# Weight loads moved into the middle of pair 14, and a second expert's turn inside the first up product, in a fused attention and expert kernel

## The chip, the cores and the metric

The kernel runs on one core of one Trainium2 chip. The metric is the device time of a whole execution in microseconds (us), the median of several runs. The profile is of one execution; its span, from the first to the last instruction, is a little shorter than the device time.

Names used below: TensorE (PE in the profile; PEld are its weight loads), VectorE (DVE), ScalarE (ACT), GpSimd (POOL), SyncE (SP). SBUF is the on-chip memory, PSUM holds the results of TensorE, DRAM is the memory outside.

## The reference

Two stages, cut to what matters here. First, attention with chunks selected per query, over 4 batches, 8 heads, 768 positions and a head size of 64; then a layer of 8 experts, each of which serves at most 80 tokens.

```python
# attention: q, k, v are (4, 8, 768, 64)
ub = upper bound of q.k over each chunk of 32 keys      # from k_min, k_max
sel = the 6 chunks with the largest ub, causal
attn = softmax(where(sel & causal, q @ k.T / 8, -1e9))
x = (attn @ v) as rows of 512, one for each of 3072 tokens

# experts: w_gate (512, 8), w1 (8, 512, 1024), w2 (8, 1024, 512)
expert_idx = argmax(x @ w_gate); gate_w = its softmax probability
out = zeros(3072, 512)
for e in range(8):
    tok_idx = tokens with expert_idx == e
    if more than 80: keep the 80 with the largest gate_w
    h = maximum(x[tok_idx] @ w1[e], 0)                  # "up"
    out[tok_idx] = gate_w[tok_idx] * (h @ w2[e])        # "down"
```

## The kernel before

Attention is worked off in 16 pairs of heads (`NP = 16`), numbered 0 to 15; four pairs make a batch. Beside the attention of one batch the kernel ranks the tokens of the batch before by their gate weight, so that after pair 15 only the last batch's ranking is left. Then come the experts. A helper `op(engine, instruction, r=..., w=...)` records what each instruction reads and writes and places the semaphore waits. Every engine works off its own instructions in program order; `"gpd"` is a DMA issued by GpSimd, `"sp"` one issued by SyncE.

The loop over pairs, cut to the order of the parts:

```python
for i in range(NP):
    kk, bb = i % NPB, i // NPB - 1      # NPB = 4; pair 14: kk = 2
    live = bb >= 0
    scores(i, 0, 2)                     # score products, exp
    ...
    folds(i, 0, 1)                      # GpSimd: causal select, adds into ES
    ...
    scores(i, 2, 4)                     # calls folds for steps 2 and 3
    if live and kk == 2:
        rank_count(bb)                  # TensorE; reads flags kept in w1s[7], w2s[6]
        rank_slot(bb)
    ...
    rows(i - 1); scale_rows(i - 1)      # token rows of pair i-1 to DRAM (x_rows)
    ...
    scores(i, 4, 6)                     # calls folds for steps 4 and 5
    ...
    values(i)                           # values product; reads steps 0,1,2,4 then 3,1,4,2,5
    if i == NP - 2:
        table(bb); merge(bb); vw_turn()
    ...
    if i == NP - 2:                     # pair 14
        wload(E - 2, 0); wload(E - 2, 1); wload(E - 1, 0)
    elif i > 1:
        wload((i - 2) // 2, i % 2)
    if i in (0, 1, 12, 13):             # zeros for a quarter of out
        ...                             # i == 0: clear the start of w1s[6]
        op("sp", lambda: sp.dma_start(zd, zs), r=[zk], w=[f"outz{g}"], ...)
```

`wload(e, 0)` loads w1 of expert e (f32 in DRAM, bf16 in SBUF, 1 MB written), `wload(e, 1)` its w2. The output's zeros are read out of a cleared part of `w1s[6]`, so w1 of expert 6 may be loaded only when the four zero writes are done. The ranking of a batch keeps flags in the buffers of w1 of expert 7 and w2 of expert 6 (`Cs`), so those may be loaded only when `rank_count` of pair 14 is done. w2 of expert 7 (`last_w2`) goes in eight pieces into buffers of q and k, and is issued near the end of pair 15.

The values product, and the selects that it waits for:

```python
# values: (key tile, first and last query, step, column)
AVS = [
  [(0, 0, 128, None, 0), (0, 128, 512, 0, 128), (1, 128, 512, 1, 0),
   (2, 256, 512, 2, 0), (3, 384, 512, 4, 0)],
  [(0, 512, 768, 3, 0), (1, 512, 640, 1, 384), (1, 640, 768, 4, 384), (2, 512, 768, 2, 256),
   (4, 512, 768, 3, 256), (3, 512, 768, 4, 128), (5, 640, 768, 5, 0)],
]
# folds: GpSimd clears the part of the diagonal above the causal line, then adds
op("gp", lambda: gp.affine_select(ad, a, ...), r=[f"E{st}"], w=[ak])          # line 544
op("gp", lambda: gp.tensor_tensor(o, in0, in1, ALU.add), ...)                 # line 553
```

After pair 15, the end of the last ranking and the experts:

```python
rows(NP - 1)
keep_warm(4)                      # four products of no use, 128 x 512 bf16
...
scale_rows(NP - 1)                # VectorE, then SyncE: last write to x_rows
gate_gcols(b)
last_count((0, 5, 1, 4, 2, 3), (0, 0, 0, 0, 0, 4))    # 2nd list: warming products after each
rank_slot(b); rank_hot(b); ...
table(b); merge(b)                # gives idx, the token indices of each expert
for e in range(3):
    gather(e)                     # GpSimd: 80 rows of x_rows by idx; waits for all writes
spread()
...
keep_warm(13)
turn(0)                           # TensorE transposes the 80 rows, ScalarE copies
gather(3)
up(0)
turn(1)
gather(4)
for e in range(1, E):
    if 1 < e + 1 < E:
        turn(e + 1)
        if e + 4 < E: gather(e + 4)
    up(e)                         # two halves of 16 products each
    if e % 4 > 0 and e != 3: down(e // 4 * 3 + e % 4 - 1)
    elif e == 4: down(2)
```

Of the kernel before, what the change touches and what calls it, by code (L numbers as in the profile page):

```python
# [5 lines left out]
ACTF = mybir.ActivationFunctionType  # L6
# [141 lines left out]
def bass_quest_chunk_select__then__topk_capacity_drop_kernel(  # L148
# [11 lines left out]
    E = moe_w_gate.shape[1]  # L160
    Fd = moe_w1.shape[2]
    Dm = moe_w_gate.shape[0]
    CAP = int(moe_capacity)
# [3 lines left out]
    DB = Dm // 128  # L167
    FB = Fd // 128
    NPB = H // 2
    NP = B * NPB  # L170
# [35 lines left out]
    with ExitStack() as pers:  # L206
# [15 lines left out]
        op = sy.op  # L222

        with nc.Block() as blk:

            @blk.sync
            def _body(_unused):
                sp = nc.sync
                gp = nc.gpsimd
                ve = nc.vector  # L230
                ac = nc.scalar
# [102 lines left out]
                def xTv(e):  # L334
                    return bass.AP(rq, (e % 2) * 160, [[S, 128], [1, 160]]).bitcast(BF16)
# [587 lines left out]
                for i in range(NP):  # L923
                    kk, bb = i % NPB, i // NPB - 1
                    live = bb >= 0
                    scores(i, 0, 2)
                    if i == NP - 1:
                        sort_rows(True)
                        vw_mm()
                        clear_xg("k", 0)  # L930
                    if i:
                        sums(i - 1)
                        scale_lg(i - 1)
                    folds(i, 0, 1)
                    if live and kk == 0:
                        gate_in(bb)
                    if live and kk == 1:
                        rank_pred()
                        rank_cmp(bb, 5)
                    scores(i, 2, 4)  # L940
                    if i == 0:
                        take_r(1)
                    if live and kk == 2:
                        rank_count(bb)
                        rank_slot(bb)
                    if live and kk == 3 and i < NP - 1:
                        table(bb)
                        merge(bb)
                    if i == 12:
                        sort_apply()  # L950
                        sort_take()
                    if i:
                        if i == NP - 1:
                            sort_rank(0)
                        rows(i - 1)
                        scale_rows(i - 1)
                    if i == NP - 2:
                        rank_late(bb)
                    if live and kk == 0:
                        gate_exp()  # L960
                        gate(bb)
                    scores(i, 4, 6)
                    if i + 1 < NP:
                        bounds(i + 1)
                    if i + 2 < NP:
                        take_q(i + 2)
                        take_r(i + 2)
                    if i + 1 < NP:
                        bounds_out(i + 1)
                    if i + 2 < NP:  # L970
                        take_k(i + 2)
                    if i + 4 < NP:
                        load(i + 4, "qk")
                    if i == NP - 4:
                        load_vk(NP - 1, 0)
                    if live and kk == 0:
                        rank_own(bb)
                    if live and kk == 1:
                        rank_diag(bb)
                        rank_cmp(bb, 4, 3, 2, 1, 0)  # L980
                    if live and kk == 2 and i < NP - 2:
                        rank_late(bb)
                    if i == NP - 1:
                        sort_rank(1)
                        last_w2()
                        break
                    if i == NP - 2:
                        op("dve", lambda: ve.tensor_scalar(triM[:], triQ[:], 1.0, 3e38, ALU.is_ge, ALU.mult), r=["triQ"], w=["triM"])
                        op("dve", lambda: ve.scalar_tensor_tensor(triM[:], ident_f[:], 3e38, triM[:], ALU.mult, ALU.max),
                           r=["triM", "ident_f"], w=["triM"])  # L990
                        for n, s in (("q", 0), ("q", 1), ("k", 1)):
                            clear_xg(n, s)
                    values(i)
                    if i == NP - 2:
                        table(bb)
                        merge(bb)
                        vw_turn()
                    if i + 2 < NP:
                        load(i + 2, "v")
                    if i + 1 < NP:  # L1000
                        unselT(i + 1)
                    if live and kk == 0:
                        rank_row(bb)
                    if i == 11:
                        sort_rows(False)
                        sort_rank()
                    if i == NP - 2:
                        wload(E - 2, 0)
                        wload(E - 2, 1)
                        wload(E - 1, 0)  # L1010
                    elif i > 1:
                        wload((i - 2) // 2, i % 2)
                    if i in (0, 1, 12, 13):
                        zk = f"w1_{E - 2}"
                        if i == 0:
                            op("dve", lambda: ve.memset(bass.AP(w1s[E - 2], 0, [[DB * Fd, 128], [1, 2 * Dm]]), 0.0), w=[zk])
                        g = (0, 1, 12, 13).index(i)
                        zs = bass.AP(w1s[E - 2], 0, [[DB * Fd, 128], [0, NT], [1, 2 * Dm]]).bitcast(F32)
                        zd = bass.AP(out.tensor, out.offset + g * NT * 128 * Dm, [[Dm, 128], [128 * Dm, NT], [1, Dm]])
                        op("sp", lambda: sp.dma_start(zd, zs), r=[zk], w=[f"outz{g}"], dsem=f"d_zero{g}")  # L1020
# [29 lines left out]
                last_high(2)  # L1050
                scale_rows(NP - 1)
                gate_gcols(b)
                last_count((0, 5, 1, 4, 2, 3), (0, 0, 0, 0, 0, 4))
                rank_slot(b)
                rank_hot(b)
                op("dve", lambda: ve.tensor_copy(dT[:, 2, :], gT[:]), r=["gT", "dT"], w=["dT"])
# [25 lines left out]
                        bounds_check=NTOK - 1, oob_is_err=False),  # L1082
                        r=XD + ["idx"] + ([f"xS{e - 3}"] if e > 2 else []), w=[xgk(e)], dsem=f"d_g{e}")

                def turn(e):
                    tp = MB if e % 2 == 0 else M0b
                    tk = "MB" if e % 2 == 0 else "M0"
                    for d in range(DB):
                        op("pe", lambda: pe.transpose(tp[:, d * CAP:(d + 1) * CAP], xgv(e)[:, ts(d)], ident_bf[0:CAP, 0:CAP]),
                           r=[xgk(e), "ident_bf"], w=[tk], inc=(d == DB - 1))  # L1090
                    k0 = ["rq"] if e < 2 else []
                    op("act", lambda: ac.activation(xTv(e), tp[:, 0:DB * CAP], ACTF.Copy), r=[tk], w=[f"xT{e % 2}", f"xS{e}"] + k0)

                def up(e):
                    s = e % 2
                    for hf in range(2):
                        for fb in range(hf * 4, hf * 4 + 4):
                            for d in range(DB):
                                o = SC[s][:, hf * 512 + (fb % 4) * CAP:hf * 512 + (fb % 4 + 1) * CAP]
                                op("pe", lambda: pe.matmul(o, w1s[e][:, d, ts(fb)], xTv(e)[:, d * CAP:(d + 1) * CAP],  # L1100
                                                           start=(d == 0), stop=(d == DB - 1)),
                                   r=[f"w1_{e}", f"xT{s}"], w=[f"H{s}{hf}", f"SC{s}"], inc=(fb % 4 == 3 and d == DB - 1))
                        src = SC[s][:, hf * 512:hf * 512 + 4 * CAP].rearrange('p (f c) -> p f c', f=4)
                        dst = hTv(e)[:, hf * 4 * HW:(hf + 1) * 4 * HW].rearrange('p (f c) -> p f c', f=4)[:, :, 0:CAP]
                        k0 = [("qT", "kT")[e // 2] + str(s)] if e < 4 and hf == 0 else []
                        if hf == 0:
                            op("act", lambda: ac.activation(dst, src, ACTF.Relu), r=[f"H{s}{hf}"], w=[f"hT{e % 4}{hf}"] + k0)
                        else:
                            op("dve", lambda: ve.tensor_scalar(dst, src, 0.0, None, ALU.max), r=[f"H{s}{hf}"], w=[f"hT{e % 4}{hf}"])
# [21 lines left out]

                for e in range(3):
                    gather(e)
                spread()
                for e in range(4):
                    t = (qT, kT)[e // 2 % 2][e % 2]
                    op("dve", lambda: ve.memset(bass.AP(t, CAP // 2, [[S, 128], [HW // 2, FB], [1, (HW - CAP) // 2]]), 0.0), w=[("qT", "kT")[e // 2] + str(e % 2)])
                keep_warm(13)
                turn(0)
                gather(3)  # L1140
                up(0)
                turn(1)
                gather(4)
                for e in range(1, E):
                    if 1 < e + 1 < E:
# [44 lines left out]
```

## Time and profile before

| | |
|---|---|
| device time, median of 3 runs | 297.52 us (297.23 to 298.48) |
| span of the profiled execution | 296.4 us |
| TensorE busy | 276.3 us (93%) |
| GpSimd busy | 227.3 us (77%) |
| VectorE busy | 210.4 us (71%) |
| ScalarE busy | 146.7 us (49%) |
| chain that ended last | TensorE 65%, GpSimd 15%, VectorE 10%, DMA 5% |
| bytes moved by DMA | 47.95 MB, 162 GB/s on average |

How to read it: the busy shares are averages over a long attention stage and a tail of experts, which have different limits. A second part of the profile page cuts the span into 40 equal slices, 7.41 us each, and gives each engine's busy share in tenths; a line PEclk gives the clock granted to TensorE in tenths of full speed, and a line DMA the busy share of the 16 DMA engines. The chain of waits follows the execution back from its last instruction to what released each step. L553 is line 553 of the kernel before; where one name stands for numbered buffers, the number is left out (`ES`, `EXB`, `w1s`). A DMA's "us to landing" is from its issue to the arrival of its last byte.

### The profile page before, as it was taken

The page shows a single profiled execution, that of the slowest core. Times are in us where ns is not written, and L with a number is a line of the kernel's source. Part 1 is how long each engine was busy: PE and PEld are TensorE (multiplying, and loading weights), DVE is VectorE, ACT ScalarE, POOL GpSimd, SP SyncE. Part 2 cuts the span into 40 slices and gives each one's busy share as a digit, 9 for nine tenths or more (in the row PEclk, how much of TensorE's full clock was granted, in tenths as well). Part 3 has the DMA queues.
Part 4 walks back from the last instruction along what each step waited for, and adds up shares of the span by engine and source line. Part 5 has one row for each costly group of instructions (what it writes and reads, how often), then busy time and mean ns, then how long its engine had stood idle before and what let it go on. Part 6 is the DMA issues. An engine that isn't in the chain of part 4 may idle for free.

```text
span 296.4 us, 8664 instructions
## 1 busy us (share of the span) xinstructions
PE 276.3 (93%) x3593; PEld 170.5 (58%) x3593; DVE 210.4 (71%) x573; ACT 146.7 (49%) x202; POOL 227.3 (77%) x297
## 2 busy tenths in 40 slices
PE   7579999999999999999999999999999999749992
PEld 7235565655656565656565656565656575327761
DVE  3767282737797989659889898898899989602431
ACT  2155646565657555545754546566656545103320
POOL 5039897989998999989899999899999924043522
PEclk9779999999999999999999999999999999877998
DMA  9997959699999899979899999997999699911211
GB/s 150 173 163 123 300 101 303 117 173 170 158 169 191 146 170 155 192 133 167 156 192 168 163 166 205 152 171 131 215 317 211 92 192 203 201 41 38 80 62 58
DMA packets 158359, 47.95 MB, mean 162 GB/s; under 512 B 142405, under 2 KB 150721, under 8 KB 158320
## 3 DMA queue, kind: packets, MB, share of 16 engines
q1 hardware_dynamic: 141664, 28.34, 48.3%
q0 software_dynamic: 13520, 18.67, 37.9%
q10 hardware_dynamic: 3136, 0.39, 0.9%
q8 instruction: 28, 0.46, 0.6%
q14 instruction: 11, 0.09, 0.1%
HBM read 53.49 MB, written 11.01 MB: 218 GB/s over the span
## 4 chain that ended last, share of the span: by engine, by line
PE 65%; POOL 15%; DVE 10%; DMA 5%; issue 2%; ACTq 1%; POOLq 0%; ACT 0%; DVEq 0%
PE SC L510 20%; PE OB L567 17%; POOL ES L553 12%; PE SC L525 4%; PE SC L1100 4%; PE M L594 4%; PE OB L1122 4%; PE OB L640 3%; DMA x_rows<-xp 3%; POOL EXB L544 3%; PE M L473 2%; PE M L580 2%; DMA kn<-in_k_dram 1%; PE MB L498 1%; DMA qn<-x_rows,idx 1%
## 5 line engine op out<-in xcount | busy, mean ns | idle before, releaser
L530 ACT ACTIVATE EXB<-SC 128x1024 f32<-128x1024 f32 x96 | 86.2, 916 | 49.4 <-PE SC L525 48.2
L553 POOL TENSOR_TENSOR ES<-ES,EXB 128x256 f32<-128x256 f32 (+1 forms) x105 | 101.6, 980 | 4.8
L510 PE MATMUL SC<-qT,kT 64*128 64x512 f32 (+3 forms) x512 | 99.2, 478 | 1.0 <-ACT EXB L530 1.0
L567 PE MATMUL OB<-EXB,vn 128*64 128x256 f32 (+3 forms) x704 | 72.8, 361 | 0.5 <-POOL EXB L544 0.5
L567 PEld LDWEIGHTS OB<-EXB,vn 128*64 128x64 f32 x704 | 46.6, 137 | 23.9 <-issue 9.5
L510 PEld LDWEIGHTS SC<-qT,kT 64*128 64x128 f32 x512 | 42.5, 191 | 25.2 <-issue 15.7
L553 POOL TENSOR_TENSOR ES<-EXB 128x768 f32<-128x768 f32 (+1 forms) x30 | 46.7, 1558 | 2.5
L525 PE MATMUL SC<-unsT,ind 64*128 64x128 bf16 (+5 forms) x256 | 38.2, 293 | 0.8 <-ACT unsT L500 0.8
L544 POOL TENSOR_SCALAR_AFFINE_SELECT EXB<-EXB 128x256 f32<-128x256 f32 x79 | 33.9, 439 | 2.5 <-ACT EXB L530 2.5
L575 ACT ACTIVATE oT<-OB 128x512 f32<-128x512 f32 (+1 forms) x32 | 15.6, 488 | 39.6 <-PE OB L567 39.6
L525 PEld LDWEIGHTS SC<-unsT,ind 64*128 64x128 bf16 x256 | 13.0, 96 | 18.5 <-issue 8.3
L441 DVE STREAM_TRANSPOSE qT<-qn 128x768 f32<-128x768 f32 x16 | 15.6, 972 | 9.2 <-PE SC L525 9.2
L585 DVE STREAM_TRANSPOSE M<-M 128x192 f32<-128x192 f32 x16 | 6.3, 394 | 21.8 <-PE M L594 21.5
L660 DVE TENSOR_TENSOR xp<-OB,rden 128x768 bf16<-128x768 f32 x16 | 15.3, 955 | 6.6 <-PE OB L640 6.3
L445 ACT ACTIVATE rq<-qT 128x768 f32<-128x768 f32 x16 | 13.5, 843 | 9.7 <-DVE qT L441 9.1
L451 DVE STREAM_TRANSPOSE kT<-kn 128x768 f32<-128x768 f32 x16 | 15.5, 967 | 3.6 <-DMA kn<-in_k_dram 3.6
L1080 POOL DMA_INDIRECT qn<-x_rows,idx x4 | 3.9, 980 | 17.4 <-DMA x_rows<-xp 14.6
L455 DVE TENSOR_REDUCE kmm<-kT 128x24 f32<-128x768 f32 x16 | 15.2, 950 | 0.5
L1128 POOL DMA_INDIRECT out_dram<-EXB,idR x6 | 6.0, 992 | 12.4 <-DVE EXB L1126 8.9
L457 POOL TENSOR_TENSOR kmm<-kmx,kmm 128x24 f32<-128x24 f32 x16 | 7.3, 454 | 10.7 <-DVE wg L904 7.0
L456 DVE TENSOR_REDUCE kmx<-kT 128x24 f32<-128x768 f32 x16 | 15.1, 942 | 0.0
L487 DVE MAX8 top<-M 128x8 f32<-128x8 f32 (+4 forms) x160 | 14.6, 166 | 0.6
(218 smaller groups left out, 417.6 us busy)
## 6 DMA issues: line engine op xcount, KB each, us to landing
w1s<-in_moe_w_dram POOLq DMA_DIRECT2D x8, 1024.0 KB, 10.1
w2s<-in_moe_w_dram POOLq DMA_DIRECT2D x7, 1024.0 KB, 11.2
qn<-in_q_dram SPq DMA_DIRECT2D x64, 96.0 KB, 3.0
vn<-in_v_dram SPq DMA_DIRECT2D x32, 192.0 KB, 3.9
out_dram<-w1s SPq DMA_DIRECT2D x4, 1536.0 KB, 7.8
kn<-in_k_dram SPq DMA_DIRECT2D x60, 96.0 KB, 2.6
x_rows<-xp SPq DMA_DIRECT2D x16, 192.0 KB, 6.4
kn<-in_k_dram ACTq DMA_DIRECT2D x4, 96.0 KB, 4.0
```

The costliest lines, as they stand in the source:

```text
L441: op("dve", lambda: ve.transpose(qT[j][:], qn[s][:].rearrange("p a b c -> p (a b c)")), r=[f"qn{s}{g}" for g in range(4)], w=[f"qT{j}"])
L451: op("dve", lambda: ve.transpose(kT[j][:], kn[s][:].rearrange("p a b c -> p (a b c)")), r=[f"kn{s}{g}" for g in range(4)], w=[f"kT{j}"])
L455: op("dve", lambda: ve.tensor_reduce(kmm[j][:, 0, 0:NCH], kv, AX, ALU.min), r=[f"kT{j}"], w=[f"kmm{j}"])
L456: op("dve", lambda: ve.tensor_reduce(kmx[:], kv, AX, ALU.max), r=[f"kT{j}"], w=["kmx"])
L510: op("pe", lambda: pe.matmul(o, kT[j][pr, ts(kt)], qT[j][pr, q0:q1], start=True, stop=False), r=[f"kT{j}", f"qT{j}"], w=[f"SC{s}"], inc=False)
L525: op("pe", lambda: pe.matmul(o, ind[pr, ts(kt)], unsT[j][pr, b0 - 128:q1 - 128], start=False, stop=True), r=[f"ind{h}", f"unsT{j}"], w=[f" ...
L530: op("act", lambda: ac.activation(Ex(st, None, 0, W), src, ACTF.Exp, scale=SCALE), r=[f"SC{s}"], w=[f"E{st}"])
L544: op("gp", lambda: gp.affine_select(ad, a, pattern=[[0, 2], [1, 128]], compare_op=ALU.is_ge, fill=0.0, base=0, channel_multiplier=-1), r=[ ...
L553: op("gp", lambda: gp.tensor_tensor(o, in0, in1, ALU.add), r=[f"E{s2}", f"E{first[0]}"] if first else [f"E{s2}"] + kt, w=kt)
L567: op("pe", lambda: pe.matmul(OB[pr, q0:q1], vn[s][:, kt, h, :], ex, start=(n == 0), stop=last), r=[f"vn{s}{h}", "ES0" if st is None else f ...
L575: op("act", lambda: ac.activation(oT[:, q0:q1], OB[:, q0:q1], ACTF.Copy), r=[f"O{bk}"], w=[f"oT{bk}"])
L660: op("dve", lambda: ve.tensor_tensor(xo, xi, rx, ALU.mult), r=["O0", "O1", "rden"], w=[f"xp{i % 2}"])
```

## The change

Four things are changed.

- The three weight loads of pair 14 (w1 and w2 of expert 6, w1 of expert 7) are issued right behind `rank_count`, in the middle of the pair, instead of at its end. They are meant to be out of the way of the last write of token rows. On GpSimd they now stand ahead of the selects of steps 4 and 5 and the six last adds of pair 14, instead of behind them.
- So that w1 of expert 6 finds its buffer free then, the zero writes go out in pairs 0, 1, 11 and 12 instead of 0, 1, 12 and 13. The part of the buffer that holds the zeros is untouched until then.
- The warming products are set anew: six instead of four after the last count, four new ones between table and spread, twelve instead of thirteen behind the spread, two new ones behind the first turn. They keep TensorE busy while it waits.
- The second expert's turn goes into the middle of the first up product, and VectorE instead of ScalarE copies its result to SBUF, so that TensorE doesn't wait for that copy.

The diff, with the parts cut that only carry these through:

```diff
                     if live and kk == 2:
                         rank_count(bb)
                         rank_slot(bb)
+                        if i == NP - 2:
+                            wload(E - 2, 0)
+                            wload(E - 2, 1)
+                            wload(E - 1, 0)
 ...
-                    if i == NP - 2:
-                        wload(E - 2, 0)
-                        wload(E - 2, 1)
-                        wload(E - 1, 0)
-                    elif i > 1:
+                    if 1 < i < NP - 2:
                         wload((i - 2) // 2, i % 2)
-                    if i in (0, 1, 12, 13):
+                    if i in (0, 1, 11, 12):
 ...
-                last_count((0, 5, 1, 4, 2, 3), (0, 0, 0, 0, 0, 4))
+                last_count((0, 5, 1, 4, 2, 3), (0, 0, 0, 0, 0, 6))
 ...
-                def turn(e):
+                def turn(e, eng="act"):
 ...
+                    if eng == "act":
+                        op("act", lambda: ac.activation(xTv(e), tp[:, 0:DB * CAP], ACTF.Copy), ...)
+                    else:
+                        op("dve", lambda: ve.tensor_copy(xTv(e), tp[:, 0:DB * CAP]), ...)
 ...
-                def up(e):
+                def up(e, mid=None):
                     for hf in range(2):
                         for fb in range(hf * 4, hf * 4 + 4):
                             ...
+                        if hf == 0 and mid:
+                            mid()
 ...
                 for e in range(3):
                     gather(e)
+                keep_warm(4)
                 spread()
 ...
-                keep_warm(13)
+                keep_warm(12)
                 turn(0)
                 gather(3)
-                up(0)
-                turn(1)
+                keep_warm(2)
+                up(0, lambda: turn(1, "dve"))
                 gather(4)
```

More of the change, by code (lines that the diff above doesn't have):

```diff
@@ L1016, in _body @@
                             op("dve", lambda: ve.memset(bass.AP(w1s[E - 2], 0, [[DB * Fd, 128], [1, 2 * Dm]]), 0.0), w=[zk])
-                        g = (0, 1, 12, 13).index(i)
+                        g = (0, 1, 11, 12).index(i)
                         zs = bass.AP(w1s[E - 2], 0, [[DB * Fd, 128], [0, NT], [1, 2 * Dm]]).bitcast(F32)
@@ L1091, in turn @@
                     k0 = ["rq"] if e < 2 else []
-                    op("act", lambda: ac.activation(xTv(e), tp[:, 0:DB * CAP], ACTF.Copy), r=[tk], w=[f"xT{e % 2}", f"xS{e}"] + k0)
-                def up(e):
+                    if eng == "act":
+                        op("act", lambda: ac.activation(xTv(e), tp[:, 0:DB * CAP], ACTF.Copy), r=[tk], w=[f"xT{e % 2}", f"xS{e}"] + k0)
+                    else:
+                        op("dve", lambda: ve.tensor_copy(xTv(e), tp[:, 0:DB * CAP]), r=[tk], w=[f"xT{e % 2}", f"xS{e}"] + k0)
+                def up(e, mid=None):
                     s = e % 2
```

## The prediction

> **What bounds the kernel now.** I began with the page: TensorE is busy for 93% of the span and holds most of the chain that ended last, so up to about 250 us a saving elsewhere counts only if TensorE waits for it. The 40 slices (7.41 us each) show where that stops being true.
>
> ```profile
> PE   7579999999999999999999999999999999749992
> PEclk9779999999999999999999999999999999877998
> DMA  9997959699999899979899999997999699911211
> ```
>
> TensorE's dip (7 and 4) and the dip of its clock begin at 259 us, in the slices where DMA has just fallen to 1. So the tail is where transfers and TensorE trade places. The chain of waits of the last 70 us, in order of time (start, us, what), gives that moment:
>
> ```profile
> 252.63 0.87 DVE xp L660
> 253.50 0.03 DVE RC L698
> 253.53 7.88 DMA x_rows<-xp
> ...
> 262.30 2.63 DMA qn<-x_rows,idx
> 264.93 0.05 issue
> 264.98 0.46 PE MB L1089 x4
> 265.44 0.02 issue
> 265.46 0.45 ACT rq L1092
> 265.90 0.05 issue
> 265.95 2.32 PE SC L1100 x32
> 268.27 0.28 PE M L1089 x4
> ```
>
> The write of the last token rows takes 7.88 us, then 0.89 us until GpSimd starts the first gather, then 2.63 us for the gather. The first turn, the first up product, the second turn and its ScalarE copy follow one after another, and the second up product ends at 271.13. From there TensorE runs without a gap to 290.62. The list of token indices was ready at 256.42 (VectorE, start 256.26 plus 0.16), so the gathers waited for the write alone.
>
> Why 7.88? I listed this write pair by pair in the DMA view. The same 192 KB took 2.4 us at 51 us and 3.8 at 38 us, in stretches where the DMA share was 0.05 to 0.75. At 253.53 the share is above 1, because weights are in flight. The DMA issues of 235.7 to 236 us (KB each, us to landing) and GpSimd's timeline say which:
>
> ```profile
> w2s<-in_moe_w_dram POOLq DMA_DIRECT2D x1, 1024.0 KB, 14.3
> w1s<-in_moe_w_dram POOLq DMA_DIRECT2D x1, 1024.0 KB, 19.0
> ...
> 226.50 1.28 POOL L553 TENSOR_TENSOR ES<-EXB 128x512 f32<-128x512 f32 x1
> 227.74 0.85 POOL L544 TENSOR_SCALAR_AFFINE_SELECT EXB<-EXB 128x256 f32<-128x256 f32 x2
> 228.57 5.64 POOL L553 TENSOR_TENSOR ES<-ES,EXB 128x512 f32<-128x512 f32 x6
> 234.15 0.77 POOL L411 DMA_DIRECT2D w1s<-in_moe_w_dram  x1
> ```
>
> Three loads of 1 MB are issued at 234.15, 234.92 and 235.79; the last of them lands near 255, and the eight pieces of the last expert's w2 (issued 243.39 to 247.07) land at 261.2 (247.07 plus 14.1). DMA is nearly idle from 232.7 to 235.7 (share 0.13) and full from 236 to 260. The row write shares that full stretch and ends with it.
>
> **What the Trainium skill says.** "DMA: Bandwidth & Descriptors", section "Issuing engines are not separate DMA queues": transfers issued by SyncE and by GpSimd run on the same 16 engines and interleave. The trace agrees: 2.4 us for the row write beside little else, 7.9 beside weights. The same page, "SWDGE vs HWDGE vs iDMA", says a transfer that casts must be issued by GpSimd, which computes its descriptors. The weights are f32 in memory and bf16 in SBUF, and the trace shows GpSimd held for 0.77, 0.89 and 0.77 us. "TensorE: Matmul & The Clock Gate", section "What's actually happening": half clock after an idle window of about 3.4 us, the windows running freely. The trace agrees in length; I cut it at that grid (columns: sum, PE busy, ..., PEclk, DMA share, GB/s):
>
> ```profile
> 250.20:253.62 3.42, 2.83 (x38) 1.66 (x37) 3.42 (x12) 2.80 (x6) 0.00 (x0) 1.00 1.14 205
> 253.62:257.03 3.41, 1.78 (x35) 0.89 (x34) 2.39 (x13) 0.00 (x0) 0.00 (x0) 1.00 1.23 202
> 257.03:260.44 3.41, 3.41 (x9) 1.22 (x8) 0.77 (x7) 0.00 (x0) 0.00 (x0) 0.50 0.99 166
> ```
>
> A window 83% busy kept the full clock, one 52% busy was followed by a half-clock window. The windows from 263.86 to 270.68 also ran at half, after one 32% busy. That is where the first two up products lie.
>
> **The change, part by part.**
>
> 1. Zero source. The two last zero writes (1.5 MB each) move one pair earlier, from pairs 12 and 13 to 11 and 12. Both had to end before the load of w1 of expert 6, which overwrites their source. The write at 217.9 landed 9.0 us later, at 226.9; now the last is issued near 205.7 and, with the 14.3 us the write there took, lands by about 220 to 223, before the load. The write that goes to 191 us fills DMA that was idle from 200.6 to 203.0 (share 0.21). Direct cost: none that I see.
>
> 2. Early loads, transfer side. They stand ahead of the last two selects of pair 14 on GpSimd, so they start at 227.74, 6.4 us earlier. Weights move at about 200 GB/s when little else runs (192 to 217 in the microseconds from 248 to 258), so 1 MB takes 5.2 us. Three take 15.6; with row traffic and what is left of expert 5's w2 they end near 245 to 248. Expert 7's w2 (5.2 us) then ends near 251 to 254. The last row write finds DMA almost empty: I take 2.7 us instead of 7.88.
>
> 3. Early loads, GpSimd side. The three issues hold GpSimd for 2.40 us (234.15 to 236.55), now ahead of the select of step 4. Values of pair 14 start at 226.29 and stream 2,816 columns in 4.69 us, 1.665 ns each; the item that reads step 4 is preceded by 1,152 columns, so TensorE needs it at 228.21. Before, that select ended at about 228.16: just in time. After, it ends at about 230.6, and TensorE stalls 2.4 us. Part is slack: the table then ends at 233.8 instead of 231.4, while VectorE only came free for it at 232.67. I follow both to the product on line 617: the gate merge ends at 235.5, scores and sort transposes end at 236.9, against 235.26 before. Net delay 1.65 us. The folds end at 236.6 instead of 234.15, in time for the sums at 237.7. Everything to the row write is a tight chain, so the write is issued at 253.53 + 1.65 = 255.2 and the indices come at 258.07.
>
> 4. Gather. The write lands at 255.2 + 2.7 = 257.9, no later than the indices. Plus 0.9 and 2.63: the first gather lands at 261.65, against 264.93: minus 3.3 us. The twelve warming products at 0.213 us end near 261.1, so they don't delay it.
>
> 5. Clock. Six instead of four warming products after the counts, and four after the table, fill the holes that brought half clock (each 0.21 us at full clock). Two more cover the ScalarE copy. I expect full clock from 253 us on; an up product is then 1.15 us, as later in the trace, instead of 2.32 and 2.07.
>
> 6. Second turn inside the first up product. Its 0.28 us of transposes stay, its copy (0.45 us on ScalarE plus two waits of 0.05) leaves the path. From the first turn to the end of the second up product took 6.15 us (264.98 to 271.13). Now the third gather limits it: gathers start 1.3 us apart, so it lands 2.6 after the first; then 0.25 for its turn and 1.15 for the product: 4.0 us. Parts 5 and 6 together: minus 2.2 us.
>
> Sum: 3.3 + 2.2 = 5.5 us. But a stall of 2.4 us can fill most of a clock window; at a random phase it leaves one under 52% busy in about three cases of four. A half-clock window then takes 3.41 us for work worth 1.7. I charge about half of that, 0.8 us, as some of the stall may be shorter than worked out. 297.5 - 5.5 + 0.8 = 292.8.
>
> **Rivals.**
>
> A: GpSimd becomes the bound in pair 14, stronger than I charge: stall plus a full half-clock window. For it: GpSimd is busy 0.92 to 1.00 in each microsecond from 217 to 237. Then 1.7 us are lost instead of 0.8, and descriptors written over a deeper queue could cost more: 294 to 295.5.
>
> B: no stall reaches the path, because TensorE or VectorE has slack I overlooked. For it: the chain ran on VectorE there (224 to 235 us), TensorE waited 0.46 us for VectorE's merge. The indices at 256.4 would then set the gathers: 290.5.
>
> C: the write is slow anyway, since DMA is full until 256 or later: the backlog of the moved zero write shifts the weights. Against it: 3 us of idle at 233 and 2.4 at 201 are filled, which ends the queue near 256 even with nothing else gained. Then the write lands at 258 rather than 257.9, and little is lost.
>
> D: the clock still falls to half at the up products. That returns about 2 us: 294.5.
>
> **Range and chances.** Base 292.0 without the clock penalty; B takes off 1.5, A or D adds 1.5 to 2.5; both adding gives 295.5. The 2% line is 291.6, just under my base, so faster by over 2% needs B or a bigger gain at the clock. Slower by 2% would need 11 us lost, and I see no such wait.
>
> **What would show each step.** The loads start at 227.7 and the last row write takes under 3.5 us (part 2). Step 4's select is the releaser of an idle of TensorE near 2.4 us in the values of pair 14, and the write is issued near 255.2 (part 3); if it is issued at 253.5, part 3 is wrong. The gather starts within 1 us of the indices (part 4). PEclk is 1.00 from 253 to the end, half near 231 if the stall throttles it (5). From first turn to the end of the second up product near 4.0 us (6). The prediction fails if the write still takes over 5 us, or if a wait for weights or zeros stops GpSimd at 227.7.

## The result, and the profile after

The changed kernel takes **292.85 us** (median of 4 runs, 292.74 to 292.91), the kernel before 297.73 us beside it (297.23 to 298.48): a ratio of 0.9834, with a 95% interval of 0.9812 to 0.9856. The span of the profiled execution falls from 296.4 to 291.1 us.

The busy shares and the clock in 40 slices, of the changed kernel:

```profile
PE   7579999999999999999999999999999699989991
PEclk9779999999999999999999999999999999999997
DMA  9997949699999799999999999999999999811211
```

Each slice is 7.28 us here. The dip of TensorE and of its clock at 259 us is gone; where DMA falls to 1, at 255 us, TensorE now stays at 8 and 9. A new dip of TensorE, a 6, stands at 226 us. The chain of waits shows both. Its columns are start, us and what:

```profile
227.74 0.79 POOL w1s L411
228.53 0.89 POOL w2s L414
229.41 0.76 POOL w1s L411
230.16 0.43 POOL EXB L544
230.60 0.04 issue
230.64 2.82 PE OB L567 x32
...
254.31 0.87 DVE xp L660
...
257.93 0.16 DVE idx L829
...
261.72 2.55 DMA qn<-x_rows,idx
264.27 0.05 issue
264.32 0.32 PE MB L1089 x4
264.63 1.15 PE SC L1103 x32
```

At the top GpSimd holds the chain: three load issues, the select of step 4, and then TensorE's values. At the bottom the write of token rows is no longer on the chain at all. The indices are, then the issue of three gathers, and the landing of the third one. (The page's chain steps from `idx` to the gathers by way of `idR`; see the end of this section.) The waits of TensorE from 205 us on give the new stall, and the DMA issues of 255 to 256 us the new write:

```profile
PE OB L567 <- POOL EXB L544: 2.2, 1, 2.2
PE MB L1089 <- DMA qn<-x_rows,idx: 0.7, 2, 0.4
```

```profile
x_rows<-xp SPq DMA_DIRECT2D x1, 192.0 KB, 2.3
```

The same 192 KB that took 7.88 us take 2.3. DMA is at a share of 0.09 from 253 to 255 us; the eight pieces of the last expert's w2 land 3.4 to 4.9 us after their issue, against 11.6 to 14.1 before.

One reading needs care. The page puts the first gather's wait down to the VectorE instruction that makes `idR`, because that one ends last before the gather starts (259.03 and 259.08). In the program the gathers stand ahead of it and wait for `idx` alone. The trace bears this out. GpSimd's queue (POOLq) executes two register moves of the gather's own line, the first at 258.2, ahead of `idR`, and the gather starts 0.9 us later. In the kernel before, the first of these moves came at 261.43, 0.02 us behind the landing of the write, and the gather again 0.9 us later (262.30). In the changed kernel:

```profile
L1080 POOLq MOVE  x2: 29/29/29, 258.2 to 258.8; - x2
```

So GpSimd was free to begin at 258.2, on `idx`, and from the end of `idx` (258.09) to the gather is 0.99 us.

### The profile page after: what moved, and what is told of

Its sections match the earlier page's. It is cut to its first block, busy times and chain, and to the rows that moved or that the text cites. A ratio compares the mean times of both kernels' runs of the same rounds, so it can differ in the third digit from the quotient of the medians.

```text
span 291.1 us, 8676 instructions
## 1 busy us (share of the span) xinstructions
PE 274.0 (94%) x3598; PEld 168.7 (58%) x3600; DVE 210.8 (72%) x574; ACT 146.4 (50%) x201; POOL 227.6 (78%) x297
## 4 chain that ended last, share of the span: by engine, by line
PE 65%; POOL 19%; DVE 7%; issue 3%; DMA 2%; ACTq 1%; POOLq 0%; DVEq 0%
PE SC L510 20%; PE OB L567 18%; POOL ES L553 13%; PE SC L525 4%; PE OB L1127 4%; PE M L594 3%; POOL EXB L544 3%; PE OB L640 3%; PE SC L1103 3%; PE M L473 2%; PE M L580 2%; PE MB L498 2%; DMA kn<-in_k_dram 1%; DMA qn<-x_rows,idx 1%; PE M L633 1%
## 5 line engine op out<-in xcount | busy, mean ns | idle before, releaser
L567 PEld LDWEIGHTS OB<-EXB,vn 128*64 128x64 f32 x704 | 46.8, 137 | 26.1 <-issue 9.2
L640 PE MATMUL OB<-ident_f,oT 128*128 128x128 f32 x96 | 13.9, 281 | 0.5 <-ACT oT L575 0.5
```

The lines of the kernel that those rows point to most:

```text
L567: op("pe", lambda: pe.matmul(OB[pr, q0:q1], vn[s][:, kt, h, :], ex, start=(n == 0), stop=last), r=[f"vn{s}{h}", "ES0" if st is None else f ...
L640: op("pe", lambda: pe.transpose(OB[:, ts(t)], oT[:, ts(t)], ident_f[:]), r=["oT0", "oT1", "ident_f"], w=[f"O{t // 4}"], inc=(t in (3, NT - ...
```

## The experiments

They were run in three groups, each on one chip with the kernel before beside it. The chips differ: the kernel before took 298.14, 299.76 and 298.68 us. So ratios to it are compared, or times within one group.

### Loads put back to the end of pair 14

```diff
-                        if i == NP - 2:          # behind rank_count
-                            wload(E - 2, 0); wload(E - 2, 1); wload(E - 1, 0)
-                    if 1 < i < NP - 2:
+                    if i == NP - 2:
+                        wload(E - 2, 0); wload(E - 2, 1); wload(E - 1, 0)
+                    elif i > 1:
                         wload((i - 2) // 2, i % 2)
```

> The changed kernel with the three weight loads put back to the end of pair 14 (zero writes still early, warming and turn as changed). Theory (the early loads free the last row write): no stall of TensorE in the values of pair 14, the row write is issued at 253.5 again, but takes 7 to 8 us beside the weights, the first gather lands near 264.9, TensorE idles for over 5 us before it and the first up products run at half clock: 296 to 297 us. Rival (the gain of the change is its warming and its turn, and the stall on GpSimd costs more than the loads bring): 291 to 293 us.

Measured: 297.29 us, ratio 0.9969 (0.9953 to 0.9985). The stall is gone, and the chain has the old shape. (The profiled execution, at 298.95 us, is the slowest of 20; its values of pair 14 begin at 227.39, 1.1 us later than in the changed kernel, and so does all that follows, the row write included, which was expected at 253.5.)

```profile
254.63 7.47 DMA x_rows<-xp
262.10 0.02 issue
262.12 0.03 POOLq L1080
...
262.99 2.69 DMA qn<-x_rows,idx
265.68 0.05 issue
265.72 0.45 PE MB L1089 x4
266.17 0.85 PE SC L885 x2
267.02 1.07 PE SC L1103 x16
```

Half an up product takes 1.07 us here and 0.58 at full clock. With the new warming and turn in place TensorE still waits 5.0 us for the first gather, and its clock falls. So the position of the loads is worth about 1.35% (0.9969 against 0.9834), some 4 us, and all the rest of the change only 0.3%. The changed kernel did not run in this group: its ratio in the two others was 0.9888 and 0.9842, by which the position would be worth 0.8% and 1.3%.

### Old warming

```diff
-                last_count(..., (0, 0, 0, 0, 0, 6))
+                last_count(..., (0, 0, 0, 0, 0, 4))
-                keep_warm(4)                     # ahead of spread
-                keep_warm(12)
+                keep_warm(13)
-                keep_warm(2)                     # behind the first turn
```

> The changed kernel with the warming products of before (four after the last count, none between table and spread, thirteen after the spread, none behind the first turn). Theory (the new ones hold the clock): a half-clock window after 257 us, in which the thirteen products take 4 to 4.7 us and end behind the landing of the first gather, and half clock in a part of the two first up products: 294.5 to 296 us. Rival (the clock stays at full anyway because the gathers come earlier and leave no long gap): 292.5 to 293.2 us.

Measured: 293.80 us (292.89 to 294.26), ratio 0.9834 (0.9786 to 0.9882). The profiled run, the one at 294.26, has a half-clock window in the tail (columns: sum, PE busy, ..., PEclk, DMA share, GB/s). The first line is the window of the stall in pair 14, which no half clock followed here; the other two are the tail:

```profile
228.55:231.96 3.41, 1.59 (x22) 1.30 (x24) 3.27 (x16) 0.60 (x1) 3.35 (x5) 1.00 1.04 160
255.86:259.27 3.41, 1.72 (x34) 1.17 (x36) 2.39 (x16) 0.00 (x0) 0.45 (x1) 1.00 0.23 57
259.27:262.68 3.41, 3.41 (x10) 1.18 (x8) 0.00 (x0) 0.00 (x0) 2.54 (x3) 0.52 0.15 40
```

The thirteen warming products take 4.44 us in it and end behind the landing of the gather: from the end of `idx` (257.83) to the first turn is 4.9 us, against 3.6 with the new warming. The gather for the fourth expert waits for the copy of the first turn and is late with it, so that TensorE reaches the fourth turn 11.07 us behind the end of `idx` (268.90), against 9.48 in the changed kernel: 1.6 us lost. The spans bear it out: 292.4 us here and 291.1 there, with `idx` 0.26 us earlier here. But up products ran at full clock (1.15 us), and the fastest run, at 292.89, is level with the changed kernel's 292.85. The median lies between both expectations. The mechanism is there in the profiled execution; that the faster ones went without it is not shown.

### Old turn

```diff
-                up(0, lambda: turn(1, "dve"))
+                up(0)
+                turn(1)
```

> The changed kernel with the second turn behind the first up product, copied by ScalarE, as before. Theory (the third gather limits the second up product): the second up product starts 0.1 to 0.3 us later, 292.9 to 293.2 us. Rival (the whole wait of 0.5 us for the copy returns, with 0.25 us more of reordering): 293.4 to 293.7 us.

Measured: 294.40 us, ratio 0.9866 (0.9820 to 0.9912), above both expectations. The profile says why: a half-clock window from 231.77 to 235.19, in front of which TensorE was 39% busy, has moved everything behind it by 1.4 us. What the turn itself does is read from the end of `idx` to the end of the second up product: 7.81 us here (259.48 to 267.29), 7.69 in the changed kernel. The turn is worth 0.12 us, because the third gather limits the second up product either way.

### Old zero writes

```diff
-                    if i in (0, 1, 11, 12):
+                    if i in (0, 1, 12, 13):
-                        g = (0, 1, 11, 12).index(i)
+                        g = (0, 1, 12, 13).index(i)
```

> The changed kernel with the zero writes in pairs 12 and 13, as before. The last of them landed at 226.9 us before the change and the loads start at 227.7, so GpSimd should hardly wait. Theory A (the move of the zeros only clears the queue): weights end 2 to 5 us later, between 255 and 258 us, and the row write issued at 255.2 lands near 258 to 259.5: 293 to 294.5 us. Theory B (the move is there for the wait alone): within 0.3 us of the changed kernel. Theory C (the zeros land later than 227.7 beside the other traffic and GpSimd waits for them): the stall of TensorE grows beyond 2.2 us by as much.

Measured: 294.09 us (292.77 to 294.63), ratio 0.9839 (0.9788 to 0.9890). The last zero write lands 9.2 us after its issue, the loads start at 227.76 with no wait, TensorE's stall is 2.3 us and the row write takes 2.6. The profiled run, at 294.63, again has half clock, from 230.72 to 234.13. The time lies in theory A's range, but not by its mechanism: DMA is at a share of 0.02 from 255 to 256 us, ahead of the row write at 256.8, and the delay is that of the half clock. The moved zeros bring nothing that these runs can show, which is theory B; a loss of a few tenths of a us would not be seen in this spread.

### The changed kernel again, and the loads behind the selects

> The changed kernel itself, on the same chip as the three that follow. The half-clock window that a stall in the values of pair 14 can set off depends on where the clock's windows lie, so two levels are possible: about 293 us without it, as measured first, and 294.3 to 294.8 us with it. If all runs stay at the lower level, the higher times of the two runs with the old turn and the old zeros have another cause.

Measured: 296.55 us, ratio 0.9888 (0.9858 to 0.9917), all four runs within 0.21 us, with half clock from 231.93 to 235.34. It is the higher level. On the same chip, the loads stood behind the two selects:

```diff
-                        if i == NP - 2:          # behind rank_count
-                            wload(E - 2, 0); wload(E - 2, 1); wload(E - 1, 0)
 # in folds, behind the select
+                        if i == NP - 2 and st == 5:
+                            wload(E - 2, 0); wload(E - 2, 1); wload(E - 1, 0)
                         for (s2, c2, q0, q1) in ADDS[st] if i < NP - 1 else []:
```

> The changed kernel with the three loads behind the selects of steps 4 and 5 and ahead of the six last adds of pair 14. Theory (the stall of 2.2 us in the values of pair 14 comes from the three loads standing ahead of the select of step 4): the stall is gone and with it any half clock near 231 us; the adds still end near 236.5, so the sums on TensorE wait for them about 0.6 us; the row write is issued near 254.2 and takes 2.3 us: 1 us less than the changed kernel without half clock, 291.5 to 292.3 us. Rival (GpSimd's adds are on the path as well, so that holding it costs the same wherever the loads stand): as the changed kernel, 292.7 to 293.2 us.

Measured: 294.08 us, ratio 0.9808 (0.9779 to 0.9837); 2.5 us under the changed kernel, which has the half clock here; by the ratio of its first runs, 0.9834, it is 0.8 us. The stall in the values is gone, and a shorter wait stands in its place:

```profile
PE M L598 <- POOL ES L557: 1.0, 1, 1.0
```

Line 598 is the sums product, waiting for GpSimd's adds: 1.0 us, where I expected 0.6. No half clock near 231 us. The theory stands, and the rival has a small part of the truth: the adds are next in line.

### Two loads behind the selects, one behind the adds

```diff
+                        if i == NP - 2 and st == 5:          # in folds, behind the select
+                            wload(E - 2, 0); wload(E - 2, 1)
 ...
                         wload((i - 2) // 2, i % 2)
+                    if i == NP - 2:
+                        wload(E - 1, 0)
```

> Two loads behind the selects of steps 4 and 5, the third behind the adds, at the end of pair 14. Theory: the adds end at 235.8, just before the sums want them at 235.9; no delay is left of holding GpSimd, the row write is issued at 253.5 to 253.6, the indices come at 256.4 and the queue is still never empty, so the weights end near 253: 1.5 to 1.8 us less than the changed kernel without half clock, 291.0 to 291.6 us. Rival (the third load, issued 6 us later, pushes the last weights behind 253.5 so that the row write takes over 4 us): 292 to 293.5 us.

Measured: 293.35 us, ratio 0.9799 (0.9760 to 0.9837): 3.2 us under the changed kernel on that chip, 1.0 us by the ratio 0.9834. The row write takes 2.4 us. In the third group:

> Two loads behind the selects, the third behind the adds, once more: 2.0% under the kernel before (1.8% to 2.3%), 0.4% under the filled stall, no idle of TensorE in the values of pair 14, row write 2.3 to 2.5 us.

Measured: 291.21 us (290.93 to 291.25), ratio 0.9748 (0.9712 to 0.9784), while the changed kernel took 294.34, its lowest run 293.01. The gain, 2.5%, is above the expected 1.8% to 2.3%. The waits of TensorE from 215 to 245 us no longer hold GpSimd:

```profile
PE OB L849 <- DVE gT L839: 0.6, 1, 0.6
```

That is the wait on VectorE's merge that the kernel before had too (0.5 us). The row write takes 2.3 us. This version beats both kernels in both groups.

### Third turn in the second up product

```diff
 for e in range(1, E):
-    if 1 < e + 1 < E: turn(e + 1); ...
-    up(e)
+    if e > 1: ahead()                            # ahead: the same turn and gather
+    up(e, ahead if e == 1 else None)
```

It stands on the kernel with two loads and one.

> As the kernel with two loads behind the selects and one behind the adds, and the third turn also goes into the middle of an up product (the second), so that TensorE need not wait for the third gather ahead of it. Theory (the second up product waits 0.4 us for the third gather): another 0.3 to 0.4 us less, 290.6 to 291.3 us. Rival (the copy of the third turn comes too late for the third up product, or the wait moves into the middle of the second): no difference.

Measured: 294.16 us, ratio 0.9810, 0.8 us more than without it. A miss: TensorE waits 1.1 us for VectorE's copy of the second turn instead. But all four kernels of that group show that copy about a microsecond late, which no kernel of the other groups with that copy does, so the run doesn't settle what the reordering is worth elsewhere.

### The stall filled

Nine warming products ahead of the product that waits for step 4.

```diff
 # in values, ahead of an item's two products
+                            if i == NP - 2 and st == 4 and bk == 0:
+                                keep_warm(9)
```

> The changed kernel once more, on the same chip as the three that follow. Two levels have been seen: 1.6% to 1.7% under the kernel before without a half-clock window behind the stall of pair 14, and about 1.1% under it with one.

> The changed kernel with nine warming products (1.9 us of TensorE at full clock) ahead of the product that waits for the select of step 4 in pair 14, so that TensorE is busy in its stall. Theory (the half-clock window near 231 us follows from the stall's idle time): no half clock between 225 and 240 us wherever the clock's windows lie, the product on line 617 starts 1.7 to 1.8 us later than in the kernel before and not 3.1 us, and the time is at the lower level, 1.6% to 1.7% under the kernel before. Rival (the half clock near 231 us comes from something else): it is there in this kernel as often as in the changed one.

Measured: changed kernel 294.34 us (294.37, 294.47, 293.01, 294.31), ratio 0.9842 (0.9799 to 0.9885); filled stall 292.77 us (294.02, 292.73, 292.69, 292.81), ratio 0.9802 (0.9766 to 0.9838). In front of and in the half-clock window of the changed kernel (upper two lines), and the same stage of the filled one (lower two):

```profile
227.48:230.89 3.41, 1.24 (x14) 0.56 (x10) 3.24 (x20) 0.55 (x2) 3.41 (x7) 0.98 0.99 151
230.89:234.30 3.41, 3.41 (x22) 2.31 (x20) 1.21 (x1) 0.60 (x1) 3.33 (x4) 0.51 1.11 208
```

```profile
228.00:231.40 3.40, 3.24 (x20) 1.37 (x17) 3.30 (x17) 1.41 (x3) 3.40 (x5) 1.00 0.93 141
231.40:234.80 3.40, 3.27 (x40) 2.25 (x39) 2.02 (x4) 0.70 (x2) 3.32 (x6) 1.00 1.07 192
```

The stretch from the first values product of pair 14 to the product on line 617 (619 in the filled kernel, 620 with two loads and one) tells the cost apart:

| kernel | from, to (us) | length |
|---|---|---|
| before | 226.29, 235.26 | 8.97 |
| changed, first profile | 226.28, 236.93 | 10.65 |
| changed, third group | 226.09, 238.39 | 12.30 |
| filled stall | 227.47, 238.10 | 10.63 |
| two loads and one | 226.18, 235.24 | 9.06 |

The stall costs 1.7 us net, the half clock that it can set off 1.65 more. The profile with busy work of no use in the stall has no half clock there. But it is no test of the remedy: of the 3.24 us of its first window 1.61 are warming products, and without them it would have been 48% busy (1.63 of 3.40), while the window 47% busy in the run with old warming was not followed by half clock either. The times lean to the theory (three of four at 292.7 to 292.8, against one of four at 293.01 for the changed kernel), but the two intervals overlap. So that filling a stall keeps the clock is not shown.

The excess of the profiled run, at 294.02, is not from this stage: its half-clock window lies at 26.5 to 29.9 us, at the start of the kernel, and the values of pair 14 begin 1.2 us late. The run with the loads put back, whose window lies at 26.1, has them 1.1 us late; in the other twelve profiles, with that window before 22 us, they begin between 225.99 and 226.30.

### Early loads and zeros alone

The two diffs of old warming and old turn together, on the changed kernel.

> The kernel before with the early loads and the early zeros alone: warming and turn as before. Theory (the loads bring nearly all): 1.2% to 1.6% under the kernel before, since the loads put back cost 1.35% and old warming and old turn cost little each while the gathers come early. Rival (warming and turn hold most of the gain once the write is short): under 0.9%.

Measured: 293.60 us (294.34, 292.91, 294.28, 292.91), ratio 0.9823 (0.9780 to 0.9866), no slower than the changed kernel of that group. The gain, 1.8%, is a little above the expected 1.2% to 1.6%, within its interval. The chain of the tail:

```profile
263.07 2.64 DMA qn<-x_rows,idx
265.71 0.05 issue
265.76 0.32 PE MB L1089 x4
266.07 1.20 PE SC L1103 x32
267.27 1.85 PE OB L1127 x32
```

From the first turn (263.11 in the timeline) to the end of the second up product is 4.16 us; it was 6.15 before and is 4.05 with all parts. With the old warming, TensorE has full clock from 253.9 us to the end of its work here. The up products had it in both profiles with old warming and early gathers, and not in the one with new warming and late gathers (loads put back): they got it from the early gathers, not from the new warming.

## Why the prediction was right

The forecast was 292.8 us, the measurement 292.85. Point by point:

| step | predicted | measured |
|---|---|---|
| loads start | 227.74 | 227.74 |
| TensorE's stall | 2.4 us | 2.2 us |
| delay at the product on line 617 | 1.65 us | 1.67 us |
| row write issued | 255.2 | 255.2 |
| row write takes | 2.7 us | 2.3 us |
| indices ready | 258.07 | 258.09 |
| first gather landed | 261.65 | 261.7 |
| first turn to second up product's end | 4.0 us | 4.05 us |
| charge for half clock | 0.8 us | 0 in this profile, 1.57 and 1.65 in two others |

**Parts 2 and 3** hold in sign and size, and the runs show their causes: with the loads put back the write takes 7.5 us, with the selects ahead of the loads the stall goes. Rival A happens, as an event: its half-clock window is there in some executions and not in others. Rival B was wrong as to the slack, since the net delay came out as worked out. Rival C didn't happen: even with the old zeros DMA was empty at 255 us. Nor did rival D: in all three profiles of the changed kernel the clock is full from 253 us to the end of TensorE's work. One sum of part 3 is off: the items of `AVS` add up to 2,688 columns and not 2,816, so a column takes 1.745 ns and step 4 is needed at 228.30 and not 228.21. In the trace TensorE stops at 228.44, and so the stall is 2.2 us and not 2.4; the delay that follows does not hang on it, since it was counted from the end of the select.

**Part 1**: the move of the zeros had no direct cost, as said; the runs show no gain either.

**Parts 5 and 6** have the right sum, 2.2 us against 2.1, with a wrong label. I put the full clock down to the new warming products. The run without them reached 4.16 us at full clock: it was the gathers coming 3.25 us earlier that closed the idle which had thrown the clock. The new warming is insurance for some positions of the clock's windows, as the run with old warming shows with 1.6 us by the fourth turn, and the second turn is worth 0.12 us.

**The charge for half clock** is why the centre fits so well, and it is partly luck. The four runs of the result have spans of 290.9 to 291.2, the lower level, and the span fell by 5.3 us, near the 5.5 of the base. The median time fell by 4.9 only. What made up for the charge is an accident: the profile of the kernel before, from which the 5.5 us were worked out, is of an execution of 298.19 us, and they were taken off the median of 297.52, 0.67 lower. From profile to profile, 298.19 to 292.85, the gain is 5.34 us, 3.25 for the gather and 2.1 for the tail. Where the window falls badly the changed kernel keeps less: 1.1% in the second group (ratio 0.9888) and 1.4% by the run at 294.37 in the third, still inside the predicted range.

## What to carry to other kernels

An early load isn't free on an engine that computes: its issue time (2.42 us for three loads here) stands in front of whatever that engine does next, so look for the next instruction that another engine is waiting for, and put the load behind it. Here the same loads placed behind two selects, and one of them behind the adds, kept the short write and gave the stall back. When idle time of TensorE is the cost, count it twice: the wait itself, and the half-speed window that may follow it.

## What the runs showed of the hardware

- The stall of pair 14 can set off half clock: of seven profiles with the unfilled stall five have a half-clock window right behind it, of six without the stall none has.
- The position of the clock's 3.41 us windows within the program differs from execution to execution: in the changed kernel the half-clock window behind the stall began at 231.93 in one profile, at 230.79 in another, and a third has none. In one group this kernel took 293.01 us once and 294.3 to 294.5 three times; the run at 294.37 has the window, the one at 293.01 has no profile. A comparison of two kernels can be decided by that. Not every gap of this size comes from this stage, as the run with the filled stall shows.
- The busy share of TensorE doesn't tell alone whether half clock follows. Behind the stall of pair 14, cut at the recorded change of the clock, windows 32% to 41% busy were followed by it (five profiles), windows 50% and 59% busy were not; but in the tail a window 54% busy was (old warming), as one of 52% was before. None of these windows was idle throughout. What makes the difference isn't settled.
- In the second group the copy of the second turn came about a microsecond late and TensorE's stream had further holes of about 0.6 us in the tail, in all four kernels and at a recorded full clock. ScalarE's copy of the first half of the first up product is late as well (1.40 to 1.51 us behind that half's first product, against 0.78 in the first profile of the changed kernel), so the delay is not VectorE's own. Its cause stays open.
